# A planned instruction order on all queues, a seven-product V and a halved start, in a linear-attention and GEGLU block

## The chip, the cores and the metric

The kernel runs on one core of a Trainium2 chip. The metric is the device time of one execution in microseconds (us). A core has five engines that run their own instruction lists in order: TensorE (PE in the profile; its weight loads are PEld), VectorE (DVE), ScalarE (ACT), GpSimd (POOL) and SyncE (SP). An engine whose next instruction is not ready waits, even if a later one is ready (below, VectorE stands 9.05 us in this way). SP does nothing here but issue DMA transfers; ACT and POOL issue some too. A queue named SPq, ACTq or POOLq is an engine's list of DMA issues.

The profile is one recorded execution. Its "span" runs from the first to the last instruction and was 1.9 us (after) to 2.9 us (before) shorter than the median time.

## The reference

`x` has 2048 tokens of 1024 features, in bf16. There are 32 heads.

```python
mod = (silu(c) @ w_mod)                       # 6 x 1024: sa, ca, ga, sb, cb, gb
h = layernorm(x) * (1 + ca) + sa
q, k, v = split(h @ wqkv)                     # 32 heads of 32
pq, pk = phi(q), phi(k)                       # phi(t) = where(t > 0, t + 1, exp(t)) + 1e-6
kv = einsum('bhsd,bhse->bhde', pk, v);  z = sum over s of pk
o = (pq @ kv) / (pq . z + 1e-6)
x = x + ga * (o @ wo)
h = layernorm(x) * (1 + cb) + sb
x = x + gb * ((gelu(h @ w_gate) * (h @ w_up)) @ w_down)   # 1024 -> 3584 -> 1024
```

## The kernel before

The work has two parts. The first ("attention" below, although it includes the layernorms and the output projection) reads x in four blocks of 512 tokens, normalizes each, computes K and V and sums `kv` over all tokens, computes Q, and then multiplies by `wo`. The second ("gate/up and down") handles two groups of 1024 tokens. Q, gate, up and down already use the seven-product form: operands are cut into 2 x 2 halves, and sums of the halves let seven half-size products stand for eight. It takes 12.5% fewer matmuls, and pays with additions on VectorE. K and V were plain products:

```python
def kv_group(b, tl, n, pk, vta, banks):               # 128 tokens, 512 columns of [K | V]
    ps = banks()
    for k in range(KD):                               # 8 products                   (L426)
        nc.tensor.matmul(ps, lhsT=hr1[b][:, k, tl * P:(tl + 1) * P],
                         rhs=Wkv[:, k, n * NW:(n + 1) * NW], start=(k == 0), stop=(k == KD - 1))
    if n < 2:
        phi(pk[:, n * NW:(n + 1) * NW], ps)           # K
    else:
        nc.scalar.activation(out=vta[...], in_=ps..., func=AF.Copy)   # V
```

The first block is transposed on TensorE. The others are normalized, written to DRAM, and read back by one transposing DMA each on the SP queue:

```python
def ln1_cols(b):
    nc.sync.dma_start_transpose(out=hr1[b], in_=xa_scr[b][:])          # (L331)
    ...
```

The 6 x 1024 modulation values come from three sets of eight w_mod tiles. Set 0 is needed before the first K; the steps of sets 1 and 2 are placed at fixed points of the block loop, one after every K/V group, so their loads come close together:

```python
ms1, ms2 = ModSet(1, wm_ring, 7), ModSet(2, wm_ring, 0)
mods = {10 + i: ms1 for i in range(KD)}
mods.update({23 + i: ms2 for i in range(KD)})
```

The language's scheduler orders most of attention and the down stage. Only part of the compute is in hand-written order:

```python
ordered = {mybir.EngineType.PE, mybir.EngineType.DVE, mybir.EngineType.Activation}
with tc.manual_schedule(engines=ordered):
    wo_phase()
    gate_up(0)
down_out(0)
... # the same for the second group
```

Last, the end of a down tile. It loads the residual rows (`x2s`, the x that attention has already updated, kept in DRAM), adds them, and stores.

```python
def finish(tl, nh, ps, sb):
    xt = xio_ring()
    nc.sync.dma_start(out=xt, in_=x2_scr[tt][:, cs])
    t = c0_ring()
    nc.vector.tensor_tensor(out=t, in0=ps, in1=sb, op=ALU.add)        # frees the PSUM bank
    nc.vector.tensor_tensor(out=t, in0=t, in1=gbrow[:, cs], op=ALU.mult)
    nc.vector.tensor_tensor(out=xt, in0=t, in1=xt, op=ALU.add)        # waits for x2s
    nc.scalar.dma_start(out=o_dram[...], in_=xt)
```

## Time and profile before

| | before |
|---|---|
| time, first three runs | 798.39 us median (796.95 to 800.98) |
| span of the profile | 794.2 us |
| first K matmul | 21.30 us |
| first gate/up matmul | 280.89 us |
| gate/up's first matmul to the end | 513.31 us, with one idle 0.86 in it |

These are lines of the first, second and fourth part of the page of the kernel before: busy time of each engine with its share of the span; then busy tenths in 40 slices of 19.9 us each, the granted TensorE clock in tenths, and the busy share of the 16 DMA engines in tenths; then the chain that ended last, by engine.

```profile
span 794.2 us, 10331 instructions
PE 763.7 (96%) x3673; PEld 346.5 (44%) x3673; DVE 551.7 (69%) x1097; ACT 323.0 (41%) x583; POOL 42.9 (5%) x108
PE   3999699999899999999999999999999999999997
DVE  4647754555989598888888889357777677747144
PEclk9999799999999999999999999999999999999999
DMA  8999900002149865755657989754323323346451
PE 83%; DMA 4%; DVE 3%; ACT 2%; issue 1%; POOL 0%; SPq 0%; DVEq 0%; POOLq 0%
```

TensorE is busy 96% of the span, so it is the bound. The 4% it is idle are not spread out: the first and fifth slices show 3 and 6, and in the fifth the clock falls to 7. Idle and slow time is thus nearly all in the first 285 us. The TensorE timeline of the kernel before shows where. Its columns are start, duration, engine, line, operation, shapes and count; in brackets, the idle time just before and what ended it.

```profile
19.12 0.25 PE L274 MATMUL psum<-mem 128*128 128x4 f16 x4 [0.80 <-DVE mem L271]
21.30 20.88 PE L426 MATMUL psum<-mem 128*128 128x512 bf16 x88 [1.93 <-DVE mem L320]
...
86.29 0.62 PE L263 MATMUL psum<-mem 128*32 128x512 bf16 x4 [4.97 <-DMA mem<-in_w_mod_dram]
86.84 3.59 PE L426 MATMUL psum<-mem 128*128 128x512 bf16 x8
...
96.20 0.25 PE L274 MATMUL psum<-mem 128*128 128x4 f16 x4 [2.09 <-DVE mem L271]
...
280.89 3.62 PE L639 MATMUL psum<-mem 128*128 128x512 f16 x16
285.37 14.85 PE L639 MATMUL psum<-mem 128*128 128x512 f16 x68 [0.86 <-DVE mem L230]
```

Three readings: the first K matmul starts at 21.30 us. At 86 us TensorE waits 4.97 us for a w_mod tile, and then eight matmuls take 3.59 us instead of the usual 1.90, because the clock has dropped. From 285.37 us on, one 512-column matmul follows another every 0.2157 us. The issues on the SP queue, from its timeline:

```profile
67.75 9.23 SPq L331 DMA_TRANSPOSE mem<-xas  x1
77.08 1.48 SPq L252 DMA_DIRECT2D mem<-in_w_mod_dram  x3
```

Issuing one transposing DMA occupied the SP queue for 9.23 us, and the w_mod loads stood behind it.

### The profile page before, as it was taken

What the parts mean: (1) busy time and instruction counts of PE and PEld (TensorE: products, weight loads), DVE (VectorE), ACT (ScalarE), POOL (GpSimd) and SP (SyncE); (2) the same over time, 40 slices, a digit from 0 to 9 for tenths busy, and PEclk for the clock granted to TensorE, in tenths of its full rate; (3) what the DMA queues carried; (4) which work ended last, traced back from release to release, by engine and by line L of the source; (5) the groups of instructions that cost most, each with busy time, mean ns of one, the idle gap of its engine ahead of it and who ended that gap; (6) DMA issues with size and microseconds to landing.
All of it is one profiled execution on the core that took longest, in us unless ns stands there. A gap on an engine that the chain in (4) does not pass through costs nothing.

```text
span 794.2 us, 10331 instructions
## 1 busy us (share of the span) xinstructions
PE 763.7 (96%) x3673; PEld 346.5 (44%) x3673; DVE 551.7 (69%) x1097; ACT 323.0 (41%) x583; POOL 42.9 (5%) x108
## 2 busy tenths in 40 slices
PE   3999699999899999999999999999999999999997
PEld 2444344545344444444444444444444444444443
DVE  4647754555989598888888889357777677747144
ACT  1635157575997045445444401004454454430100
POOL 1101000000034100000000140000000000000000
PEclk9999799999999999999999999999999999999999
DMA  8999900002149865755657989754323323346451
GB/s 325 382 327 286 268 1 1 1 1 64 43 118 287 232 196 162 211 146 173 198 147 225 305 256 249 242 172 128 99 61 106 87 73 106 120 160 190 141 166 46
DMA packets 148194, 129.12 MB, mean 163 GB/s; under 512 B 34992, under 2 KB 129712, under 8 KB 148144
## 3 DMA queue, kind: packets, MB, share of 16 engines
q1 hardware_dynamic: 140016, 112.74, 48.4%
q0 software_dynamic: 3520, 11.54, 3.8%
q10 hardware_dynamic: 4608, 4.20, 1.7%
q8 instruction: 28, 0.46, 0.2%
q14 instruction: 22, 0.18, 0.1%
HBM read 98.04 MB, written 23.07 MB: 152 GB/s over the span
## 4 chain that ended last, share of the span: by engine, by line
PE 83%; DMA 4%; DVE 3%; ACT 2%; issue 1%; POOL 0%; SPq 0%; DVEq 0%; POOLq 0%
PE psum L639 42%; PE psum L741 21%; PE psum L426 7%; PE psum L359 6%; PE psum L575 5%; DMA mem<-xas 2%; DVE mem L230 2%; DMA mem<-xhs 1%; PE psum L441 1%; PE psum L499 1%; DMA xas<-mem 1%; PE psum L512 0%; DVE mem L333 0%; ACT mem L340 0%; ACT mem L501 0%
## 5 line engine op out<-in xcount | busy, mean ns | idle before, releaser
L639 PE MATMUL psum<-mem 128*128 128x512 f16 x1568 | 339.0, 379 | 0.9 <-DVE mem L230 0.9
L639 PEld LDWEIGHTS <-mem 128*128 128x128 f16 (+1 forms) x1568 | 153.3, 98 | 186.2 <-DVE mem L230 1.4
L230 DVE TENSOR_TENSOR mem<-psum,mem 128x512 f16<-128x512 f32 (+2 forms) x261 | 174.8, 681 | 77.0 <-PE psum L639 38.2
L364 ACT ACTIVATE mem<-psum 128x512 f32<-128x512 f32 x208 | 122.3, 595 | 216.6 <-PE psum L639 146.6
L230 DVE TENSOR_TENSOR mem<-mem 128x512 f16<-128x512 f16 (+7 forms) x378 | 191.3, 542 | 23.7 <-ACT mem L340 5.7
L741 PE MATMUL psum<-mem 128*128 128x512 f16 (+1 forms) x784 | 169.5, 379 | 0.0
L426 PE MATMUL psum<-mem 128*128 128x512 bf16 x512 | 121.1, 387 | 1.9 <-DVE mem L320 1.9
L741 PEld LDWEIGHTS <-mem 128*128 128x128 f16 x784 | 76.7, 98 | 92.5
L651 ACT ACTIVATE mem<-mem 128x512 f16<-128x512 f16 x84 | 52.9, 629 | 94.7 <-DVE mem L230 94.7
L426 PEld LDWEIGHTS <-mem 128*128 128x128 f16 x512 | 49.3, 99 | 63.3 <-issue 7.5
L575 PE MATMUL psum<-mem 128*128 128x512 f16 x256 | 56.9, 379 | 3.4 <-ACT mem L340 2.0
L359 PE MATMUL psum<-mem 128*128 128x512 f16 x224 | 54.5, 380 | 0.1
L288 DVE BATCH_NORM_STATS2 mem<-mem 128x6 f32<-128x512 bf16 x64 | 40.7, 669 | 3.5 <-DMA mem<-in_A_x_dram 2.5
L575 PEld LDWEIGHTS <-mem 128*128 128x128 bf16 x256 | 25.0, 98 | 35.1 <-issue 5.3
L338 ACT ACTIVATE mem<-psum 128x512 f16<-128x512 f32 x40 | 24.1, 603 | 32.0 <-PE psum L426 31.6
L753 DVE TENSOR_TENSOR mem<-psum,mem 128x512 f16<-128x512 f32 x24 | 16.5, 689 | 29.4 <-PE psum L741 29.4
L341 DVE TENSOR_SCALAR mem<-mem 128x512 f16<-128x512 f16 x56 | 15.9, 288 | 30.3 <-ACT mem L338 29.2
L359 PEld LDWEIGHTS <-mem 128*128 128x128 f16 (+1 forms) x224 | 21.9, 98 | 27.2 <-issue 2.0
L432 ACT ACTIVATE mem<-psum 128x512 f16<-128x512 f32 x32 | 19.0, 595 | 31.3 <-PE psum L426 31.2
L340 ACT ACTIVATE mem<-psum 128x512 f16<-128x512 f32 x40 | 24.1, 604 | 0.0
L501 ACT ACTIVATE mem<-psum,mem 128x512 f32<-128x512 f32 x32 | 21.7, 680 | 0.1
L503 ACT ACTIVATE mem<-mem 128x512 bf16<-128x512 f32 x32 | 20.2, 633 | 3.5 <-DVE mem L230 2.8
(80 smaller groups left out, 307.4 us busy)
## 6 DMA issues: line engine op xcount, KB each, us to landing
mem<-in_B_w_gate_dram SPq DMA_DIRECT2D x28, 512.0 KB, 4.4
mem<-in_B_w_up_dram SPq DMA_DIRECT2D x28, 512.0 KB, 5.9
mem<-ts SPq DMA_DIRECT2D x112, 128.0 KB, 3.1
mem<-in_w_mod_dram SPq DMA_DIRECT2D x24, 512.0 KB, 9.1
mem<-in_B_w_down_dram SPq DMA_DIRECT2D x6, 1792.0 KB, 7.7
mem<-in_A_x_dram SPq DMA_DIRECT2D x32, 256.0 KB, 3.5
mem<-in_B_w_down_dram SPq DMA_DIRECT2D x14, 512.0 KB, 6.4
ts<-mem SPq DMA_DIRECT2D x14, 512.0 KB, 3.4
```

Of the source, the lines that this page charges most:

```text
L230: nc.vector.tensor_tensor(out=out, in0=a, in1=b, op=op)
L288: nc.vector.bn_stats(out=stats[:, cb, :], in_=xt[:, cb * BW:(cb + 1) * BW])
L338: nc.scalar.activation(out=e, in_=t, func=AF.Exp)
L340: nc.scalar.activation(out=r, in_=t, func=AF.Relu)
L359: nc.tensor.matmul(ps, lhsT=w[:, k, j * P:(j + 1) * P], rhs=h[:, k, :], start=(start and k == 0), stop=(k == KH - 1), skip_group_check=True)
L364: nc.scalar.activation(out=t, in_=ps, func=AF.Copy)
L426: nc.tensor.matmul(ps, lhsT=hr1[b][:, k, tl * P:(tl + 1) * P], rhs=Wkv[:, k, n * NW:(n + 1) * NW], start=(k == 0), stop=(k == KD - 1))
L501: nc.scalar.activation(out=lnd, in_=psd, func=AF.Ln, bias=eps6, scale=1.0)
L575: nc.tensor.matmul(psw, lhsT=pqT[b][:, g, tl * P:(tl + 1) * P], rhs=Wp[:, g, cs], start=(g == 0), stop=(g == KD - 1))
L639: nc.tensor.matmul(ps, lhsT=a[:, u, k, :], rhs=b[:, k, :], start=(start and k == 0), stop=(k == KH - 1), skip_group_check=True)
L651: nc.scalar.activation(out=t, in_=src, func=AF.Gelu_apprx_tanh)
L741: nc.tensor.matmul(ps, lhsT=a[:, i, q * P:(q + 1) * P], rhs=b[:, i, :], start=(start and i == 0), stop=(i == NPR - 1), skip_group_check=True)
```

## The change

The intent is to remove matmuls from V, to start sooner, and to take the waits out of the attention part by deciding the order of every instruction at build time. It has four parts.

1. V takes the seven-product form, within a block of 512 tokens (224 matmuls instead of 256). Some of the activation sums are shared with Q.
2. The start handles 256 tokens, then the other 256. 25 matmuls whose results nobody reads ("fillers", `keep_warm`) keep TensorE busy before the first K.
3. Every engine call is recorded, not executed. A planner gives each a modelled duration, keeps TensorE's order as written, list-schedules the other engines forwards and backwards several times, and then issues everything in that one fixed order, DMA issues included.
4. The second group's transposing DMAs move from the SP to the ACT queue. Gate/up and down keep their matmuls.

```diff
+class Plan:
+    def add(self, eng, name, args, kw, line):      # records a call, and what it depends on
+    def cost(self, op, outs, ins):
+        ...
+        elif op.fn.startswith("dma"):
+            op.cost, op.bytes = 1000 if op.eng == "POOL" else 60, ...
+            if op.fn == "dma_start_transpose":
+                op.bytes = 3584 * 360
+                op.cost = 6000 if op.eng == "ACT" else 60          # ns
+    def issue(self):
+        with self.tc.manual_schedule():
+            for op in self.order():                # the planned order, all five engines
+                ...
...
+    def keep_warm(n, cols):
+        for _ in range(n):
+            te.matmul(psD()[:, 0:cols], lhsT=ident, rhs=..., start=True, stop=True, ...)
...
-            nc.scalar.activation(out=vta[:, g0:g0 + NW // P, 0:P], in_=..., func=AF.Copy)
+    def v_stages(b):                               # seven stages, 4 products x 2 each
+        ...
+        return seven(mm, comb, direct)
...
-    mods = {10 + i: ms1 for i in range(KD)}
-    mods.update({23 + i: ms2 for i in range(KD)})
+        for i in range(KD):
+            put(1, 2 * i, ms1.step)                # spread over two blocks,
+            put(2, 4 + 2 * i, ms2.step)            # through a ring of two slots
...
-            nc.sync.dma_start_transpose(out=hr2[:, :, h * TG:(h + 1) * TG], in_=xh_scr[g][h][:])
+            (ac if g else sy).dma_start_transpose(out=hr2[:, :, h * TG:(h + 1) * TG], in_=xh_scr[g][h][:])
...
-    with tc.manual_schedule(engines=ordered):
-        wo_phase()
-        gate_up(0)
-    down_out(0)
+    wo_phase(kvq_phase())
+    gate_up(0)
+    down_out(0)
+    ...
+    plan.issue()
```

## The prediction

> **What bounds the kernel now.** TensorE. The page shows PE busy 763.7 of 794.2 us, and the chain of waits is 83% PE. The loss is not spread evenly. From 285.4 us to 789.9 us (gate/up and down) the chain is PE without a gap, one 512-column matmul every 0.2157 us. The first 285 us (attention and the first layernorms) hold about 247 us of matmuls at that pace, by counting groups; some 38 us are idle or slow there. The PE timeline places them: start, first K matmul only at 21.30 us (about 15 lost: x and w_mod loads, layernorm); 20 to 30 us, granted clock 0.71 then 0.95, about 2 lost; 81 to 96 us, waits of 4.97 and 2.09 plus a re-warm (granted clock 0.50; eight matmuls 3.59 us instead of 1.90), about 9; 211 to 223 us, waits for ACT, about 4; 272 to 285 us, waits for DVE, about 2.
>
> **What the change does.**
> 1. V gets the seven-product form: 224 instead of 256 matmuls, 32 x 0.2157 = 6.9 us less PE, all on the chain. It costs DVE about 4.1 us of additions per 512 tokens (six at 0.69) plus 5.5 us of weight sums; the activation sums are shared with Q. Twelve normalizations of 0.54 us move to ACT. DVE is 46 to 60% busy between 100 and 200 us, so this should hide, less surely before 50 us.
> 2. The start is halved: two x tiles before w_mod, then 256 tokens; 25 filler matmuls keep TensorE busy. The Trainium skill ("TensorE: Matmul & The Clock Gate", Part 1) says that idle halves the clock and about 3.4 us of work restores it; this trace agrees (0.50 at 85 to 90 us). I expect first K at about 19 us, 2 to 3 saved, and the slow matmuls after it gone; the second half's evacuation gives about 1.5 back.
> 3. All instructions, DMA issues included, are put in one fixed order from a model of durations. w_mod steps are spread through two blocks on a ring of two slots. That should remove most of the 9 us near 85 us and the 2 us near 275.
> 4. Gate/up and down keep their matmuls and PE order: about 504 us again.
>
> **Sum.** First K at 19.2, then about 236 us of attention matmuls: gate/up could start at 255 where it now starts at 281. All stalls gone would give a span of 767. I expect about 10 us of stalls to stay: 1.5 in the start, up to 3 at the second block (first transposed tokens), 2 to 4 for w_mod, 2 to 4 where ACT makes the denominators. The SP queue spends 5.0 to 9.2 us issuing one transpose in this trace while the change's model takes 0.06; w_mod loads queued behind the second transpose may come late, as they do now (issued 77.1, first used 86.3).
>
> Predicted: span 775, time **777 us** (now 798.4), 8 in 10 between **766 and 792**. Faster by over 2% 0.66, within 2% 0.31, slower 0.03.
>
> **What would show it.** K/V matmuls 288 + 224; PE timeline: first K at 18 to 20 us; granted clock near 1 from 20 us on; no w_mod wait over 3 us; gate/up starting at 260 to 268 us; from there to the end still 508 to 510 us; DVE busy up by 15 to 25 us.
>
> **What would make it wrong.** A fixed order built from wrong durations stalls an engine at the head of its queue: DVE (86% busy in gate/up) late with PSUM, SP blocked behind a transpose, or the second group's transposes, now issued on the ACT queue, holding ACT. Then gate/up and down lengthen and the gain shrinks to 1%. If the model is good the stalls nearly vanish: 768.

## The result, and the profile after

The changed kernel gives the right output. It took 781.82 us (median of 12 runs, 778.55 to 787.01); the kernel before, run beside it, took 797.14 us (15 runs). The ratio is 0.981, with a 95% interval of 0.9784 to 0.9835: 1.9% less time, on either side of the 2% line. Ratios here are the mean time of one kernel's fast runs over that of the other's fast runs of the same rounds, so they are not quite the ratio of the medians quoted beside them. Spans: 794.2 before, 779.9 after.

The same parts of the page, of the changed kernel:

```profile
span 779.9 us, 10339 instructions
PE 759.3 (97%) x3666; PEld 342.8 (44%) x3666; DVE 564.7 (72%) x1145; ACT 330.4 (42%) x575; POOL 54.4 (7%) x120
PE   6899999998999999999999999999999999999997
DVE  3995856759999877788888783697777777646144
PEclk9999999999999999999999999999999999999999
DMA  9947861031449832447676889962332323356561
PE 89%; DVE 6%; DMA 2%; ACT 1%; issue 1%; SPq 0%; DVEq 0%; ACTq 0%
```

The hole in the fifth slice is gone, and so is the drop of the clock there. The DMA engines, full in the first five slices before, now have room from the third slice on: the same 129.12 MB are spread over a longer stretch. TensorE's busy time fell by 4.4 us. V's missing matmuls (6.9 us less) and the fillers (8.8 us more, in the groups by line) alone would have raised it by 1.9; the other 6.3 us are not accounted for line by line, but matmuls at a dropped clock, like the eight at 86 us, counted as longer before. The TensorE timeline after:

```profile
19.84 3.93 PE L763 MATMUL psum<-mem 128*128 128x512 bf16 x16 [0.19 <-DVE mem L551]
...
28.72 9.02 PE L763 MATMUL psum<-mem 128*128 128x512 bf16 x41 [0.42 <-ACT mem L554]
...
190.46 0.38 PE L785 MATMUL psum<-mem 128*128 128x512 bf16 x1 [0.53 <-DVE mem L800]
...
265.05 35.13 PE L1014 MATMUL psum<-mem 128*128 128x512 f16 x162
...
434.26 63.62 PE L1116 MATMUL psum<-mem 128*128 128x512 bf16 x294
499.57 21.31 PE L1116 MATMUL psum<-mem 128*128 128x512 f16 x98 [1.69 <-DVE mem L1128]
...
528.52 16.78 PE L1014 MATMUL psum<-mem 128*128 128x512 f16 x77 [0.73 <-ACT mem L635]
```

Gate/up starts 15.84 us sooner (265.05 against 280.89). From there to the end it takes 514.85 us instead of 513.31, so 1.54 us are given back: the old idle of 0.86 is gone, and idles of 1.69 and 0.73 us are new, inside stretches where the kernel before never stopped. 15.84 - 1.54 is the whole 14.3 us of span.

Where do the 15.84 us come from? An estimate from the matmuls that each trace has between the first K and gate/up, at 0.2157 us for 512 columns and a quarter of that for the w_mod matmuls, which use 32 of the 128 columns of TensorE: 236.2 us of work before and 230.2 after (V's 32 matmuls less, the transposes of the start's second half more). These stretches took 259.59 and 245.21 us. So 1.46 us come from the earlier first K, 6.0 from the work, and 8.4 from lost time (waits, gaps and slow clock), which fell from 23.4 to 15.0 us. Near 86 us the old kernel lost 4.97 + 2.09 us of waits and 1.69 us to the clock, and in the new one no matmul waits for w_mod at all. Of the 15.0 us that the new attention part still loses, some 1.8 are idle time between the two halves of the start (25 to 29 us), and some 3.9 lie between 185 and 201 us (57 matmuls, worth 12.29 us, in 16.16), with idles of 0.2 to 0.5 as in the L785 line, where VectorE and ScalarE are both over 90% busy making `Wp` (`kv` times `wo`) and the denominators.

### Where the new idle in the down stage comes from

The line at 499.57 says that TensorE waited 1.69 us for VectorE's L1128, the addition that frees a PSUM bank (PSUM is the memory that TensorE writes to). That is not yet the cause. VectorE's own timeline of the changed kernel, a little earlier:

```profile
493.52 0.42 DVE L1130 TENSOR_TENSOR mem<-mem 128x512 bf16<-128x512 f16 x1 [9.05 <-DMA mem<-x2s]
```

VectorE stood 9.05 us at the head of its list with an addition whose residual rows (x2s) had not come; the bank-freeing additions were behind it. The timelines of the SP and the ACT queue of the changed kernel show why the rows were late:

```profile
470.09 19.47 SPq L1111 DMA_DIRECT2D mem<-ts  x10
489.61 0.43 SPq L1123 DMA_DIRECT2D mem<-x2s  x1
...
471.25 11.80 ACTq L910 DMA_TRANSPOSE mem<-xhs  x1
```

Ten weight loads that normally take about 0.4 us each to issue took 19.47 us, and the x2s load came after them. The waits of the SP queue between 436 and 512 us name the holder (total us, times, longest):

```profile
SPq L1111 <- DMA mem<-xhs: 12.8, 1, 12.8
```

SP waited 12.8 us for the *completion* of the transpose that ACT had issued (`xhs`), though its own load has no use for that data. In the built program the DMAs of SP and ACT take their completion semaphores in turn from the same eight, and a DMA that reuses one waits for the DMA that had it last: in the trace, the transpose completes on semaphore 103, and SP's next load on 103 was held from 475.9 to 488.72 us. So moving the transposes to the ACT queue did not take them out of SP's way.

It put them in ScalarE's way as well. From the timeline of all engines of the changed kernel:

```profile
483.15 0.60 ACT L635 ACTIVATE mem<-psum 128x512 f32<-128x512 f32 x1 [14.80 <-PE psum L1116]
483.78 0.69 DVE L1168 TENSOR_TENSOR mem<-psum,mem 128x512 f32<-128x512 f32 x1 [3.23 <-ACT mem L635]
```

This PSUM copy on ScalarE started just after the transpose's issue ended (471.25 + 11.80); with the transposes on SP (e5) it starts at 471.42. The view names PE because it counts no DMA issue as busy time. VectorE waited 3.23 us for the copy, and then the 9.05 us for x2s. Since x2s came last, SP's wait set the end here.

### The profile page after: what moved, and what is told of

It is laid out like the page before. It is cut to its first block, busy times and chain, and to the rows that moved or that the text cites. A ratio compares the mean times of both kernels' runs of the same rounds, so it can differ in the third digit from the quotient of the medians.

```text
span 779.9 us, 10339 instructions
## 1 busy us (share of the span) xinstructions
PE 759.3 (97%) x3666; PEld 342.8 (44%) x3666; DVE 564.7 (72%) x1145; ACT 330.4 (42%) x575; POOL 54.4 (7%) x120
## 2 busy tenths in 40 slices
DMA packets 147154, 129.12 MB, mean 166 GB/s; under 512 B 34976, under 2 KB 127648, under 8 KB 147104
## 4 chain that ended last, share of the span: by engine, by line
PE 89%; DVE 6%; DMA 2%; ACT 1%; issue 1%; SPq 0%; DVEq 0%; ACTq 0%
PE psum L1014 43%; PE psum L1116 19%; PE psum L939 7%; PE psum L763 6%; PE psum L730 5%; PE psum L702 5%; DVE mem L472 2%; PE psum L494 1%; DVE mem L521 1%; DMA mem<-x2s 1%; DMA mem<-in_A_x_dram 1%; PE psum L544 1%; PE psum L774 1%; PE psum L785 1%; DVE mem L800 1%
## 5 line engine op out<-in xcount | busy, mean ns | idle before, releaser
L472 DVE TENSOR_TENSOR mem<-psum,mem 128x512 f16<-128x512 f32 (+2 forms) x285 | 191.2, 681 | 71.9 <-ACT mem L635 35.0
L635 ACT ACTIVATE mem<-psum 128x512 f32<-128x512 f32 x232 | 137.0, 595 | 226.0 <-PE psum L1014 131.3
L472 DVE TENSOR_TENSOR mem<-mem 128x512 f16<-128x512 f16 (+6 forms) x398 | 202.2, 533 | 22.8 <-DMA ts<-mem 3.7
L1116 PE MATMUL psum<-mem 128*128 128x512 f16 (+1 forms) x784 | 169.7, 379 | 1.7 <-DVE mem L1128 1.7
L1116 PEld LDWEIGHTS <-mem 128*128 128x128 f16 x784 | 76.7, 98 | 94.3 <-issue 2.0
L763 PE MATMUL psum<-mem 128*128 128x512 bf16 x256 | 60.6, 380 | 1.3 <-DVE mem L551 0.9
L702 PE MATMUL psum<-mem 128*128 128x512 f16 (+1 forms) x224 | 52.0, 379 | 0.7 <-ACT mem L635 0.7
L763 PEld LDWEIGHTS <-mem 128*128 128x128 f16 x256 | 24.6, 98 | 33.1 <-DVE mem L551 2.9
L623 ACT ACTIVATE mem<-psum 128x512 f16<-128x512 f32 x40 | 23.8, 596 | 36.1 <-PE psum L763 35.8
L528 POOL TENSOR_SCALAR mem<-mem 128x1 f32<-128x1 f32 x28 | 8.6, 307 | 364.0 <-DVE mem L523 363.9
L702 PEld LDWEIGHTS <-mem 128*128 128x128 f16 x224 | 20.8, 98 | 27.4 <-issue 4.7
L1128 DVE TENSOR_TENSOR mem<-psum,mem 128x512 f16<-128x512 f32 x24 | 16.5, 686 | 18.0 <-PE psum L1116 18.0
L625 ACT ACTIVATE mem<-psum 128x512 f16<-128x512 f32 x40 | 23.8, 595 | 0.0
```

The source lines that it names most:

```text
L472: ve.tensor_tensor(out=out, in0=a, in1=b, op=op)
L623: ac.activation(out=e, in_=t, func=AF.Exp)
L625: ac.activation(out=r, in_=t, func=AF.Relu)
L635: ac.activation(out=t, in_=ps, func=AF.Copy)
L702: te.matmul(ps, lhsT=A[:, k, i * P:(i + 1) * P], rhs=B[:, k, :], start=(start and k == 0), stop=(k == KH - 1), skip_group_check=True)
L763: te.matmul(ps, lhsT=hr1[b][:, k, tl * P:(tl + 1) * P], rhs=Wk[:, k, n * NW:(n + 1) * NW], start=(k == 0), stop=(k == KD - 1))
```

## The experiments

The theory after reading the traces: (a) the gain is V's matmuls plus the waits which the planned order removes; (b) the loss behind 265 us comes from the transposes on the ACT queue, through SP and x2s. The rivals: the plan and not V makes it all, or the fillers do; and the late idles are an accident of a fixed order that moves whenever anything moves. All kernels gave right results. Unless said otherwise, each ran three or five rounds beside the kernel before. A profile is of one execution (for e5 and e9 the slowest of their fast runs, 784.05 and 795.85 us), and the change's own twelve fast runs lie 8.5 us apart, so differences of 1 or 2 us between profiles of two kernels are hints.

| run | median us | ratio to before (95%) | first K | first gate/up |
|---|---|---|---|---|
| the change | 781.82 | 0.981 (0.9784 to 0.9835) | 19.84 | 265.05 |
| e1_plain_v | 784.83 | 0.9851 (0.981 to 0.9892) | 18.95 | 269.21 |
| e2_record_order | 975.39 | 1.2238 | | 399.8 |
| e3_no_fill | 792.8 | 0.9951 (0.9914 to 0.9989) | 19.27 | 265.72 |
| e4_x2s_early | 783.69 | 0.9844 | | 265.11 |
| e5_tr_on_sync | 782.59 | 0.9794 (0.977 to 0.9818) | | 264.85 |
| e6_tr_on_sync_no_fill | 787.59 | 0.9858 (0.9834 to 0.9882) | 20.40 | 267.11 |
| e7_compute_as_written | 921.75 (one run) | | | |
| e8_start_order | 785.96 | 0.9841 | 22.89 | 267.7 |
| e9_residual_on_pool | 793.27 | 0.9935 | | 264.60 |
| e10_gate_weights_on_pool | 793.12 | 0.9936 | | 276.96 |
| e11_before_wmod_on_pool | 799.51 | 1.0014 (0.9991 to 1.0037) | | |
| e12_true_transpose_cost | 788.34 | 0.9885 (0.9853 to 0.9918) | 21.31 | 271.24 |

### e1: V as plain products, all else planned

```diff
-        return seven(mm, comb, direct)
+        def plain(tl, n):                         # 8 products, evicted by ScalarE
+            ...
+        order = [(tl, n) for tl in (2, 3, 0, 1) for n in range(2)]
+        ...
-            put(0, 2 + i, F(h_sum, 0, j), WV(j, 0), WV(j, 1))
+            put(0, 2 + i, F(h_sum, 0, j))         # no sums of V's weights
```

> The changed kernel with V computed by the plain form again (256 instead of 224 matmuls; the activation sums stay, since Q uses them; the V weight sums and the V additions go). Theory A (TensorE bounds the attention stage nearly everywhere, so removed matmuls count in full): the gate/up stage starts 6.9 us later than the 265.2 us of the changed kernel, at 271 to 273 us, and the time is about 788.5 us. Theory B (the seven-product form pays for its matmuls with vector work that stalls the first block and the ACT and DVE bound places): gate/up starts at 265 to 268 us, the time stays within 2 us of 781.8.

The V matmuls took 58.8 us instead of 52.4. From the first K to gate/up it took 250.26 us, against 245.21 with the seven products: 5.05 us, of the 6.9 that the missing matmuls are worth. The remainder, about 2 us, is lost in the first block, where the changed kernel has waits that e1 lacks: 0.31 and 0.42 us at 26 to 29 us and 0.69 us for ScalarE's L635 at 47 us. That V's extra additions cause them is likely, but not shown. In the whole time even less shows (784.83 against 781.82, with intervals that overlap), since e1 happens to have only 0.18 us idle from gate/up on. Even with plain V, gate/up starts 11.68 us before the old kernel's. The TensorE timeline of e1 (its down stage is L1126) has the first down stage in one piece:

```profile
269.21 31.03 PE L1024 MATMUL psum<-mem 128*128 128x512 f16 x143
...
439.01 84.77 PE L1126 MATMUL psum<-mem 128*128 128x512 bf16 x392
```

Here too the transposes are on the ACT queue, SP waited 8.3 us for one, and VectorE 9.0 us for x2s; it just did not reach TensorE. So that wait alone does not decide whether TensorE stops; the slack in front of it does.

### e2 and e7: the order as written, and the planned DMA order with the compute as written

```diff
-            for op in self.order():
+            for op in self.ops:                   # e2: the order in which the calls were written
```

> The changed kernel with the planner's reordering off: every engine executes in the order in which the source issues its operations; TensorE's order is the same as before. Theory A (much of the gain is the planner's reordering of VectorE, ScalarE and the DMA issues): gate/up starts 10 us or more later than 265.2 us and the down stage of the first group stalls too, since there the source puts 12 us of VectorE work in one lump; time 800 us or more. Theory B (the gain is the seven-product V, the halved start and the new places of the w_mod steps; the reordering adds little): gate/up starts before 270 us, time below 790 us.

975.39 us. The waits of TensorE of e2 are everywhere, for DMA and for compute alike, and the mean clock was 0.915:

```profile
PE psum L1116 <- DMA mem<-ts: 35.6, 12, 17.1
PE psum L702 <- ACT mem L635: 23.4, 1, 23.4
PE psum L494 <- DMA mem<-in_w_mod_dram: 18.1, 1, 18.1
```

In e7 the planner lets DVE, ACT and PE run as written and plans only the DMA issues of SP and POOL:

```diff
-        seq = [op for op in ops if op.eng == "PE"]
+        fixed = ("PE", "DVE", "ACT")
+        seqs = {e: [op for op in ops if op.eng == e] for e in fixed}
```

> The changed kernel with VectorE and ScalarE (and TensorE) in the order of the source, and only the DMA queues planned. Theory A (the reordering of VectorE and ScalarE is what the written order needs, since it puts whole blocks of layernorm ahead of urgent work): most of the 194 us that the unplanned kernel lost stays, time above 880 us. Theory B (the loss came from DMA issues standing in each other's way on the sync queue): time below 820 us.

921.75 us, one run, so of unknown state; beside steps of 50 us and more that does not matter. Its largest waits are for VectorE and ScalarE:

```profile
PE psum L705 <- DVE mem L475: 30.6, 2, 19.0
PE psum L705 <- ACT mem L638: 23.3, 1, 23.3
```

Ordering the DMA issues is worth about 54 us (975 to 922), ordering VectorE and ScalarE about 140 more (922 to 782). This measures the planner against its own recording, not against the old kernel: there, the language's scheduler did that work for most of attention. It shows that the change's source order is no order to run, and that the plan is what makes the change possible.

### e3: no fillers

```diff
-        for _ in range(n):
+        for _ in range(0):
```

> The changed kernel without the 25 filler matmuls in the start; all else is re-planned by the same rules. Theory A (the fillers keep TensorE's clock up): the first K matmuls run at half clock for about 3 us as in the kernel before (granted clock about 0.7 in the stretch 20 to 25 us), first K at 19 to 20 us, gate/up starts 1.5 to 3 us later, time 783 to 785 us. Theory B (the w_mod matmuls and transposes suffice, or other waits of the start hide it): clock near 1 from 20 us on, gate/up within 0.5 us of 265.2.

I compared the order of every other instruction with the changed kernel's: it is the same, row for row, on all engines. The fillers do what they are for, but it is little: without them the first 16 K matmuls took 5.31 us instead of 3.93, and gate/up started 0.67 us later. Yet the time rose by 11 us (10.1 between the two profiles). From the TensorE timeline of e3, then its SP waits between 436 and 512 us:

```profile
19.27 5.31 PE L763 MATMUL psum<-mem 128*128 128x512 bf16 x16 [2.01 <-DVE mem L551]
...
504.19 25.92 PE L1116 MATMUL psum<-mem 128*128 128x512 f16 x112 [8.65 <-DVE mem L1128]
```

```profile
SPq L1111 <- DMA mem<-xhs: 21.0, 1, 21.0
```

The same idle as in the changed kernel, at the same line, is 8.65 us instead of 1.69. The transpose took 17.32 us to issue on the ACT queue (11.80 in the changed kernel), SP waited 21.0 us for it (12.8), and VectorE waited 7.67 us for ScalarE's copy (3.23) and 13.5 us for x2s (9.05). The 10.1 us between the profiles are nearly all named: 6.96 here, about 1.6 because the 112 matmuls after this idle ran partly at a low clock (25.92 us instead of 24.3), 0.82 more idle at the second group's gate/up (1.55 against 0.73), and the 0.67 of the start. A fixed order has no way round a transfer that is late.

One warning about reading: the page's clock row shows full clock in the first slices of e3, although the first K matmuls there took 0.33 us each. A clock that is not full before the first long work is seen in the duration of matmuls, not in that row.

### e4: the residual rows earlier in the plan

```diff
+            plan.early = 12000.0
             sy.dma_start(out=xt, in_=x2_scr[tt][:, cs])
+            plan.early = 0.0
```

> The changed kernel with the loads of the residual rows for the outputs asked for 12 us earlier in the plan; the attention and first gate/up stages keep their order exactly. Theory A (the new stalls of 1.7 and 0.7 us between 497 and 529 us come from VectorE waiting at the head of its queue for these loads, which the sync queue issued behind a weight load that waited 3.3 us): both stalls go, from the gate/up start to the end 512.4 instead of 514.7 us, time about 779.5 us. Theory B (VectorE is simply overloaded there by the normalization of the second group): the stalls stay within 0.5 us.

A miss. The plan moves the loads, and the idle of 1.69 us does go, but VectorE still waits 9.0 us for x2s in one place, SP still waits 11.2 us for the transpose, and TensorE now stops 0.24, 1.43 and 1.64 us at 525 to 530 us, where the second group's gate/up begins. VectorE works there without a gap from 511 to 530 us; that this is the backlog from its wait for x2s is argued, not tested. The time, 783.69, is the same as the change's within the intervals.

### e5 and e6: the second group's transposes on the SP queue, with and without fillers

Nothing is planned anew: the transposes keep their place in the plan and are issued by SP.

```diff
-                self.calls[op.line](getattr(self.engines[op.eng], op.fn), op.args, op.kw)
+                self.calls[op.line](getattr(self.engines["SP" if op.fn == "dma_start_transpose" else op.eng], op.fn), op.args, op.kw)
```

> The changed kernel, planned exactly as it is, but the two transposes of the second group are issued on the sync queue, at the place in time that the plan gave them on the ScalarE queue; the order of every other instruction on every engine is the same. Theory A (two queues that issue DMAs at once hold each other up: the transpose took 11.8 us to issue on ScalarE while the sync queue needed 19.5 us for ten small loads, so the residual loads and VectorE come late): the transposes issue in 4 to 7 us each as in the kernel before, VectorE's 9 us wait for residual loads near 484 us shrinks below 4 us, the 1.7 us stall of TensorE in the down stage goes, gate/up start to end 513 us or less, time about 779.5 us. Theory B (the issuing queue does not matter, the planned order of VectorE does): the stall stays at 1 us or more.

The TensorE timeline of e5:

```profile
434.90 84.77 PE L1116 MATMUL psum<-mem 128*128 128x512 bf16 x387
519.51 6.21 PE L1014 MATMUL psum<-mem 128*128 128x512 f16 x28
526.71 1.02 PE L1014 MATMUL psum<-mem 128*128 128x512 f16 x4 [0.99 <-DVE mem L1128]
529.37 163.96 PE L1014 MATMUL psum<-mem 128*128 128x512 f16 x752 [1.64 <-ACT mem L635]
```

The down stage runs unbroken, and SP's wait for a transpose fell from 12.8 to 0.6 us. VectorE's longest wait for x2s fell from 9.05 to 5.1 us (theory A had said below 4), but its waits for x2s between 436 and 540 us still add up to 11.9 us (12.0 in the changed kernel). The first transpose now occupies SP itself for 10.08 us, and the lost time comes back a little later, where the second group's gate/up begins: 0.99 and 1.64 us. These are no price of the move alone: e4, with the transposes on the ACT queue, has idles like them at the same place. After that, 752 matmuls take 163.96 us, where the changed kernel takes 162.47: the two stops cost the clock as well (granted 0.90 and 0.76 in the two 5 us windows from 525 us on, 1.00 in the changed kernel). The time is the same as the change's.

> The kernel without fillers, with the same move of the two transposes to the sync queue. Without fillers the start itself lost only 0.5 us, but TensorE stood 8.7 us in the down stage although the order of every other instruction was the same row for row. Theory A (the 17.3 us transpose issue on ScalarE made that stall): it goes, time within 1.5 us of the run with fillers and the move. Theory B (something else of the shifted time, not the transposes' queue): a stall over 4 us stays.

e6 is e5 without fillers. The 8.65 us idle of e3 is gone (0.53 and 0.72 us in that stage), and 792.8 became 787.59. This fits the transposes on the ACT queue as the cause of e3's large idle, though the start moved too (first K at 20.40 instead of 19.27), so a mere shift in time is not excluded. The runs whose compute is planned, taken together, point the same way: in the first down stage the four runs with these transposes on SP (e5, e6, e8, e12) and the kernel before have idles of at most 0.72 us, the six with them on ACT (the change, e1, e3, e4, e9, e10) between none and 15.26. But e6 is 5.0 us slower than e5: 2.3 us of it is a late start (the first K waited 2.01 us for its weights, then ran cold), much of the rest is again idles at the second group's gate/up: 1.10, 0.24, 1.43 and 1.64 us. Without the ACT queue in play, removing the fillers still cost more than the cold matmuls did; by which path is not shown.

### e8: another order of the first K groups

```diff
-        k0 = [K(0, tl, n) for n in range(2) for tl in range(TT)]
+        k0 = [K(0, tl, n) for tl, n in ((0, 0), (1, 0), (0, 1), (1, 1), (2, 0), (3, 0), (2, 1), (3, 1))]
```

with the second half of the start and V's sums one step later, and e5's edit.

> The run with the transposes on the sync queue, and in the first block the K groups in another order: the first two token tiles do both column halves before the second two tiles, and the transposes of the second two come after three groups, so that their evacuation runs beside the fourth. Theory A (1.8 us of the wait at 25 to 29 us is TensorE standing for the second half's evacuation): these waits go, gate/up starts 1.5 to 2 us earlier. Theory B (the stage is bound later, by VectorE or the transposed tokens of the second block): gate/up starts less than 0.5 us earlier.

Miss, and confounded: the planner, given another order, put four more x tiles ahead of the first half of K's weights, and the first K waited 4.06 us for those weights (22.89 us). What the order alone is worth stays open. It does show that the start hangs on the order of the loads.

### e9 and e10: residual rows on the GpSimd queue; then weight scaling on GpSimd too

```diff
-            sy.dma_start(out=xt, in_=x2_scr[tt][:, cs])
+            gp.dma_start(out=xt, in_=x2_scr[tt][:, cs])                    # e9 and e10
-            tt_op(Wo_sb[:, kd, :].bitcast(F16), Wo_sb[:, kd, :], garow, ALU.mult)
+            gp.tensor_tensor(out=Wo_sb[:, kd, :].bitcast(F16), in0=..., in1=garow, op=ALU.mult)   # e10
```

> The changed kernel with the residual rows of the output loaded from the GpSimd queue instead of the sync queue; ScalarE's order is untouched, the sync queue keeps its order without these 32 loads, VectorE's order moves in some 17 places of the down stages. Theory A (the new stalls after the down stage of the first group come from VectorE standing at the head of its queue for residual rows, which stand on the sync queue behind weight loads that wait for TensorE): VectorE's waits for residual rows (13.2 us in sum) fall below 5 us, TensorE's stalls of 1.7 and 0.7 us go, gate/up start to end 513 us or less, time 779 to 780 us. Theory B (VectorE has too much work in that stretch whatever the loads do): stalls of 1.5 us or more in sum stay there.

This was to free the residual rows from SP's wait. It made things worse, 793.27 us. The TensorE timeline of e9:

```profile
497.58 22.73 PE L1116 MATMUL psum<-mem 128*128 128x512 f16 x96 [15.26 <-DVE mem L1168]
```

The loads left the GpSimd queue in time (at 475.5 to 478 us), but the loads between 436 and 512 us landed after 13.6 us (median; 3.9 in the changed kernel), while the transposes were in flight, which themselves landed after 17.7 us (9.7). VectorE waited 20.95 us. The Trainium skill ("DMA: Bandwidth & Descriptors", section "Issuing engines are not separate DMA queues") says that DMAs of all issuing engines run on the same 16 DMA engines and interleave, and that another issuer saves only sequencer time. This run agrees: the issue was on time and the landing was late.

> The run before this one, and the eight multiplications of the attention output weights by the gate row (0.68 us each on VectorE between 173 and 190 us) moved to GpSimd. Theory A (VectorE bounds the stretch 185 to 201 us, where TensorE loses about 4 us): TensorE loses 2 us or less there and gate/up starts 1.5 to 2.5 us earlier. Theory B (ScalarE, which makes the denominators, bounds it, or the slow GpSimd delays the weights): gate/up starts no more than 0.5 us earlier, or later.

Gate/up came 12 us later (276.96 against 265.05). The eight multiplications took 18.04 us on GpSimd, and TensorE waited 3.59 and 4.12 us for VectorE between 176 and 191 us and then ran slow. VectorE's load in that stretch cannot be shed that way. The late idle was 1.6 us this time, not 15: one more sign that its size follows from small shifts in time.

### e11: the kernel before, with its late w_mod set on another queue

```diff
-                    nc.sync.dma_start(out=wm, in_=w_mod[...])
+                    (nc.gpsimd if s == 2 else nc.sync).dma_start(out=wm, in_=w_mod[...])
```

> The kernel before with the w_mod loads of the third set issued from the GpSimd queue, so that they no longer stand behind the transpose on the sync queue; the kernel's own scheduler then also places some matmuls otherwise. Theory A (the 9 us lost between 81 and 96 us came from the sync queue: transpose issue of 9.2 us first, w_mod loads after): the 5 us wait for w_mod goes, the kernel gains 4 to 8 us, time 790 to 794 us. Theory B (the DMA engines are full there, so the loads land as late from any queue, or the transposed tokens of the third block arrive too late anyway): a gain of less than 2 us, with the wait moved to the transposed tokens.

The wait of 4.97 us for w_mod is gone (the 0.9 us for w_mod that remain are at 17.7 us, as before), and the time stayed (ratio 1.0014, 0.9991 to 1.0037). The TensorE timeline of e11 shows what took its place, then VectorE's shows why:

```profile
76.61 0.27 PE L274 MATMUL psum<-mem 128*128 128x4 f16 x4 [9.12 <-DVE mem L271]
```

```profile
70.53 1.22 DVE L230 TENSOR_TENSOR mem<-mem 128x2048 f16<-128x2048 bf16 x1 [8.87 <-DMA mem<-in_A_wqkv_dram]
```

VectorE stood 8.87 us with the sums of Q's weights, which the scheduler had placed ahead and whose load was late. It was not issued late: it left SP at 49.41 us (62.22 before) but took 21.1 us to land (11.8 before), with the DMA engines full (busy share 1.04 between 50 and 70 us) and the w_mod loads among the traffic. The third block's K began at 102.47 us, against 101.68. So the wait in the profile was real, and removing it alone is worth nothing: the load behind it was late as well. The change spreads these loads, so that its DMA engines have a busy share near 0.5 between 40 and 60 us. That this spreading, and not the order of the weight sums or of the w_mod steps, is what removed the wait was not tested alone.

### e12: plan again with a truer cost for a transpose on SP

```diff
-                op.cost = 6000 if op.eng == "ACT" else 60
+                op.cost = 6000 if op.eng == "ACT" else 5000
...
-            (ac if g else sy).dma_start_transpose(...)
+            sy.dma_start_transpose(...)
```

> Edit: the second token group's transposes are issued on the SP queue, as in e5, and the planner's cost of issuing a transpose there is 5 us (traces of this case: 4.2 to 17) instead of 0.06, so that the whole plan is worked out again with it. Theory A (the lost 2 to 3 us of the down stage come from this one wrong duration; a plan that knows it places the residual loads and the weight loads around it): gate/up starts at 264 to 266 us, gate/up's start to the end is at most 513.0 us with no PE wait over 0.8 us in it, time 778 to 780. Theory B (any fixed order from a model leaves one to three stalls of 1 to 2 us somewhere; a better duration only moves them): 781 to 786, with new waits over 0.8 us after gate/up's start or before it.

Theory B of this text, and worse than its range: 788.34 us. The TensorE timeline of e12:

```profile
21.31 3.61 PE L763 MATMUL psum<-mem 128*128 128x512 bf16 x15 [1.48 <-DMA mem<-in_A_wqkv_dram]
...
534.37 164.15 PE L1014 MATMUL psum<-mem 128*128 128x512 f16 x752 [2.12 <-ACT mem L635]
```

The truer number made another plan from the first microsecond: K's weights were issued behind more x tiles, the first K came 1.5 us later, and three idles of 1.1 to 1.6 us before 31 us, with a clock of 0.50 from 30 to 35 us, help to bring gate/up to 271.24. The down stage ran unbroken, but an idle of 2.12 us came at the second group's gate/up, with 1.7 us of slow matmuls behind it. The windows of e12 (window, its length, busy us and count of PE, PEld, DVE, ACT, POOL, then clock, DMA share, GB/s) show the clock:

```profile
530.00:535.00 5.00, 2.88 (x13) 1.21 (x12) 4.50 (x9) 1.60 (x3) 0.00 (x0) 0.97 0.26 65
535.00:540.00 5.00, 5.00 (x18) 1.91 (x17) 2.30 (x4) 2.60 (x5) 0.00 (x0) 0.69 0.00 0
```

In the second window TensorE is 5.00 us busy but does 18 matmuls instead of 25. No version I ran beats the change beyond the intervals; e5 equals it.

## Why the prediction was right or wrong

The time was right: 777 predicted, 781.82 measured, inside 766 to 792. The odds leaned too far: 0.66 for more than 2% faster, where the measured gain of 1.9% lies on the line.

- "What bounds the kernel now": right. The lost time was in the first 285 us. Gate/up starts 15.84 us sooner: about 6.0 of it is matmul work that is gone, the rest lost time and the earlier start.
- "V ... 32 x 0.2157 = 6.9 us less PE, all on the chain": the matmuls went (480 K and V matmuls instead of 512), but e1 shows 5.05 us of them between the first K and gate/up. About 2 us went to waits in the first block. "288 + 224" was a miscount: it is 256 + 224.
- "First K at about 19 us, 2 to 3 saved, and the slow matmuls after it gone": 19.84, so 1.46 saved. The first 16 K matmuls took 3.93 us, against 3.61 at full clock. The fillers matter less for this than the text suggests: e3 puts them at 0.67 us at gate/up's start.
- "Most of the 9 us near 85 us": right, all of it; no wait for w_mod is left. The reason given, the w_mod steps and their queue, was too small a part of the cause: e11 moved those loads alone and gained nothing. The text left out that the DMA engines were full there.
- "About 10 us of stalls to stay": gate/up starts at 265.05, within 260 to 268, but partly by luck. 265.05 - 19.84 - 236 would leave 9.2 us of stalls, yet 236 is what the old kernel's matmuls come to in the count above; the changed kernel's are 230.2, and 15.0 us are lost. (Some 2 of these are no stall: a group of four w_mod matmuls takes 0.33 us where its columns are worth 0.22.) The two errors nearly cancel. The division was off too: none for w_mod (2 to 4 expected), 1.8 in the start (1.5), 3.9 where the denominators are made (2 to 4).
- "From there to the end still 508 to 510 us": wrong, and this is the step that failed. It was read off from 285.4 us, where TensorE's unbroken chain begins, but gate/up's first matmul is at 280.89; without the idle of 0.86 the old figure from there is 512.45. The floor of 767 had used about 512, so the text contradicts itself. Measured: 514.85.
- "Span 775": 767 plus 10 is 777. With the text's own terms and its 2 us from span to time, it would have said 779.
- What then remains, 2.4 us, is the new idles of 1.69 and 0.73 us in the down stage and the gate/up behind it. "What would make it wrong" had named both parts of the mechanism, "the second group's transposes, now issued on the ACT queue" and VectorE late with PSUM, without giving them a term in the sum. The transposes did hold ACT's compute, as that text had it (VectorE waited 3.23 us for it), but they also held SP's loads from the other queue, which it had not, and that wait ended last. e3 shows that such an idle can reach 8.65 us, and e5 that with the transposes on SP the idles move and the time stays.
- "DVE busy up by 15 to 25": 13.0. ScalarE rose 7.4 and GpSimd 11.5, which was not predicted.
- "If the model is good the stalls nearly vanish: 768" did not come. e4, e8 and e12 each gave the model a nudge and each traded its idles for others.

On the clock, the Trainium skill ("TensorE: Matmul & The Clock Gate", Part 1) says that the full clock is lost after idle and takes about 3.4 us of work to return, and that the window which is watched is free-running. The traces fit both: before, 4.97 us idle at 86 us was followed by eight matmuls in 3.59 us. And the length of an idle alone does not decide: the kernel before had one of 2.04 us at 218 us, after which 16 matmuls took 3.61 us, full speed; in e12 an idle of 2.12 us was followed by clock 0.69, although the page's table asks for an idle window of about 3.4 us.

What stays open: why issuing one transposing DMA of the same size held its queue for 3.7 us in one place (e7) and 17.3 in another. In the changed kernel and e3 the orders are identical and the figures are 11.80 and 17.32; e5 had 10.08 on SP, e1 6.18 on ACT. Also open is what share of a transpose's delay is due to other traffic; an experiment without the other traffic would need the loads to be elsewhere in time, and the ones I tried (e4, e9) changed the traffic itself. And the parts of the change other than V were not separated: no run has the halved start or the spread w_mod loads without the plan, or the plan without them.

## What to carry to other kernels

Name the place where a stretch is measured from, and use the same one in the sum: the four microseconds between "first matmul" and "unbroken from here" were as large as anything left to predict. Before trusting a wait in the profile as a cost, ask what comes next in line: e11 removed a real wait of 5 us and gained nothing, since with full DMA engines another load became late in its place. And a fixed order of everything, planned from modelled durations, together with loads spread in time and an earlier start, won some 10 us in a part full of waits, but it passes any late transfer on to every engine behind it; taking 25 useless matmuls out of the first 20 us cost 7 us at 500 us with the order of all other instructions unchanged.

## What the Trainium skill lacked or had wrong

- "DMA: Bandwidth & Descriptors", section "DMA Transpose (X-bar)": it gives no time for which issuing a transpose of this size holds its queue. Here one 1 MB transpose held SP or ACT for 3.74 (e7) to 17.32 us (e3), while a plain load took about 0.4 us to issue.
- The same page, section "Silent corruption: two transposing streams in flight at once", says when transposes of two queues must wait for each other; and its rules say that a transpose next to ordinary DMAs needs nothing. That is about correct data. No page says what it costs plain loads: here SP's loads waited 12.8 us (the change) and 21.0 us (e3) for the completion of a transpose on ACT, because the built program shares completion semaphores between the two queues, and 0.6 us when it was on SP (e5). Nor what it costs the issuing engine's own work: ScalarE's next copy started at 483.15 us instead of 471.42 (the change, e5).
- The same page, section "Issuing engines are not separate DMA queues", holds here; what it lacks is a size for the interleaving: beside a transpose, 128 KB loads from the GpSimd queue landed after 13.6 us instead of 3.9 (e9).
- "TensorE: Matmul & The Clock Gate", Part 1: its table has the full clock lost after at least one idle window of about 3.4 us. Here 2.12 us of idle after full work were enough (e12, clock 0.69 in the next window), and 2.04 us were not (before, 218 us). Of traces it warns that their clock events can be unreliable; it does not name this case: the clock row reads 1.00 where the first 16 K matmuls of e3 took 5.31 us.
